# Shifting both stacks of SBUF tiles of an fp32r feed-forward kernel to round addresses

## The chip, the cores and the metric

One NeuronCore of a Trainium2 chip runs the program. The metric is the device time of one execution in microseconds (us). TensorE (PE) multiplies, VectorE (DVE) and ScalarE (ACT) work on single elements, GpSimd (POOL) fills constants, SyncE (SP) issues transfers. A matmul has two operands in SBUF: the stationary one, which a weight load (LDWEIGHTS, engine PEld) puts into the array, and the moving one, which streams through it column by column; the sum goes to PSUM.

## The reference

Linear attention without a softmax, then two feed-forward layers on 2304 tokens of 512 features:

```python
kv  = np.einsum('bhsd,bhse->bhde', k, v)          # batch 4, 8 heads, 576 positions, 64 wide
out = np.einsum('bhsd,bhde->bhse', q, kv)
x   = out / np.sqrt(np.mean(out * out, -1, keepdims=True) + 1e-06) * g_norm   # to (2304, 512)
h   = x @ w_in                                    # 512 to 2048
x   = (h * np.clip(h + 3.0, 0.0, 6.0) / 6.0) @ w_out
p   = domain_probs / (domain_probs.sum(-1, keepdims=True) + 1e-09)
for e in range(4):                                # experts: 512 to 1024 to 512
    out2 += p[:, e:e + 1] * (np.maximum(x @ w1[e], 0.0) @ w2[e])
```

## The kernel before, in words

Everything is float32. For the two feed-forward layers each operand is split into a high and a low part of type fp32r, and three products stand for one: high by high, high by low, low by high.

The work has three stages. The attention (to about 80 us) goes over eight pairs of a batch and half of its heads: q is transposed on PE (L208, `pq`), k and v are multiplied (L221, `kvp`), q by that product (L246, `po`), the result is normalized and transposed back (L304, `px`) into the tiles `xH` and `xL`. The first layer (to about 500 us) goes over 16 slices of 128 hidden features, grouped in units of 2, 4, 4 and 6, and five blocks of tokens (four of 512, one of 256): 12 matmuls of the input product (L333 to L335, moving `xH` or `xL`, stationary `w`), then 12 of the output product (L356, moving `gH` or `gL`, stationary `w`), three items late so that ACT and DVE can make `gH` and `gL` in between. The expert layer goes over three passes of 768 tokens, four experts and four groups of 256 hidden features; its input product is done with seven products instead of eight (L677, 384 columns, moving `xs`, stationary `win`), and the output product of the group before (L632, 512 columns, moving `wout`, stationary `g2`) fills in between.

SBUF is filled by two stacks. Pools open from the lower end in the order of the code, those with `side="right"` from the upper end downwards; a pool's tiles lie one behind the other, each rounded up to 32 bytes. So a pool's first byte is the sum of what was opened before it. The slices that the matmuls of the two feed-forward layers read begin at multiples of 512 bytes within their tile (128 weights, 384 or 512 columns, of 4 bytes each), so a whole tile has one residue. In the built program the first bytes within a partition are:

| tile | read by | role | first byte before (past a multiple of 512) | after |
|---|---|---|---|---|
| `ident`, `kvbd` | L208, L304; L246 | | 1152 (128); 2400, 3424 (352) | not moved |
| attention inputs in `accp` | L208, L221 | both | 4544 and on by 8192 (448) | 5120 and on (0) |
| `gH`, `gL` | L356 | moving | 45504 to 59840 (448) | 46080 to 60416 (0) |
| `xH`, `xL` | L333 to L335 | moving | 66368 to 131904 (320) | 66560 to 132096 (0) |
| `xs` | L677 | moving | 66368 to 125760 (320) | 66560 to 125952 (0) |
| `win` | L677 | stationary | 135136, 149472 (480) | 134144, 148480 (0) |
| `w` | L333 to L335, L356 | stationary | 163808 to 221152 (480) | 162816 to 220160 (0) |
| `g2` | L632 | stationary | 172000 to 212960 (480) | 171008 to 211968 (0) |
| `wout` | L632 | moving | 180192, 196576 (480) | 179200, 195584 (0) |

The order of the instructions on each engine is made when the program is built, by a scheduler that goes by its own estimate of times; a change in the first instructions can so move others later.

Of the kernel before, what the change touches and what calls it, by code (L numbers as in the profile page):

```python
# [8 lines left out]
F32 = mybir.dt.float32  # L9
# [8 lines left out]
def kernel(  # L18
# [18 lines left out]
    nc = tc.nc  # L37
# [3 lines left out]
    P = 128  # L41
# [18 lines left out]
    NA = NW - UNITS1[0]  # L60
    LAG = 3
    FMAX = 3.0e38

    const = ctx.enter_context(tc.tile_pool(name="const", bufs=1))
    accp = ctx.enter_context(tc.tile_pool(name="accp", bufs=NB))
    gp = ctx.enter_context(tc.tile_pool(name="gp", bufs=4))
    rp = ctx.enter_context(tc.tile_pool(name="rp", bufs=2))
    sp = ctx.enter_context(tc.tile_pool(name="sp", bufs=1))
    wp = ctx.enter_context(tc.tile_pool(name="wp", bufs=1, side="right"))
    xp = ctx.enter_context(tc.tile_pool(name="xp", bufs=1))  # L70

# [16 lines left out]
    def bank_b(shape, name):  # L88
        turn["b"] += 1
        pool, tag = (psc, "c") if turn["b"] % 6 == 0 else (psb, "b")  # L90
        return pool.tile(shape, F32, tag=tag, name=name)

    ident = const.tile([P, P], F32, name="ident")
    three = const.tile([P, 1], F32, name="three")
    gcol = const.tile([P, 1], F32, name="gcol")
# [162 lines left out]
    def att_rms(i):  # L258
# [6 lines left out]
        def scale():  # L265
            for g, tt in enumerate(banks(b)):
# [13 lines left out]
            lambda: nc.vector.scalar_tensor_tensor(  # L280
                out=w1_, in0=va, scalar=FMAX, in1=r0, op0=ALU.min, op1=ALU.mult),
            lambda: nc.vector.tensor_tensor(out=w1_, in0=w1_, in1=r0, op=ALU.mult),
# [424 lines left out]
    def run(g):  # L707
        return lambda: next(g, None)
# [20 lines left out]
    for k in range(NQ):  # L729
        ci, co = convert_in(k + 1) if 0 < k and k + 1 < NQ else iter(()), convert_out(k)  # L730
        side = [run(co), run(co), run(ci), run(ci), run(ci), run(ci), run(ci)]
# [41 lines left out]
```

## Time and profile before

| | |
|---|---|
| median of 3 runs | 1254.34 us (1251.5 to 1254.65) |
| profiled execution | 1252.49 us; span of its instructions 1250.7 us |
| mean granted clock of TensorE | 0.995 |
| PE, PEld busy | 1235.1, 1079.2 us |
| DVE, ACT, POOL busy | 767.6, 538.9, 1.3 us |
| matmuls | 6205 |

A record of a matmul lasts from its start until its last result is out, and the next one starts before that; so a PE that is always busy says nothing of how fast matmuls follow each other. The distance between starts does.

### The profile page before, as it was taken

The numbers are of one execution on the slowest core, as the hardware profiler recorded it, in microseconds if no ns is written. First come the engines' busy times: TensorE is split into PE (matmuls) and PEld (weight loads), VectorE is DVE, ScalarE is ACT, GpSimd is POOL, SyncE is SP. The second block draws the span as 40 slices with busy tenths as digits, with TensorE's granted clock in tenths as the row PEclk, the third lists the DMA queues.
The fourth block names the chain that finished last, engine by engine and source line by source line (L and its number), as shares of the span: only waits on it lengthen the run. The fifth ranks groups of instructions, "written<-read, shape, count | busy, mean of one in ns | idle before, by whom it ended". The sixth has DMA issues, their size and how long they took to land.

```text
span 1250.7 us, 15739 instructions
## 1 busy us (share of the span) xinstructions
PE 1235.1 (99%) x6205; PEld 1079.2 (86%) x6205; DVE 767.6 (61%) x1489; ACT 538.9 (43%) x1049; POOL 1.3 (0%) x10
## 2 busy tenths in 40 slices
PE   8899999999999999999999999999999999999998
PEld 6778888888888889999999999999999999999997
DVE  3989996693533465565656595656565856555553
ACT  5766753452322433333333353344444544444431
POOL 0000000000000000000000000000000000000000
PEclk9989999999999999999999999999999999999999
DMA  9932331120010002021111122122121222121111
GB/s 253 223 98 68 102 101 34 51 68 1 1 68 1 1 1 68 34 68 68 68 68 68 68 101 85 68 68 68 68 69 68 93 93 68 68 68 68 68 34 51
DMA packets 63897, 87.02 MB, mean 70 GB/s; under 512 B 5200, under 2 KB 47184, under 8 KB 63824
## 3 DMA queue, kind: packets, MB, share of 16 engines
q1 hardware_dynamic: 63664, 86.03, 22.3%
q8 instruction: 48, 0.79, 0.3%
q14 instruction: 25, 0.20, 0.1%
q10 hardware_dynamic: 160, 0.00, 0.0%
HBM read 81.30 MB, written 4.72 MB: 69 GB/s over the span
## 4 chain that ended last, share of the span: by engine, by line
PE 95%; DMA 2%; DVE 2%; ACT 1%; issue 0%; SPq 0%; DVEq 0%; ACTq 0%
PE po L632 32%; PE qa L677 16%; PE po L356 16%; PE qb L677 12%; PE ph L335 5%; PE ph L333 5%; PE ph L334 5%; DMA vin<-in_v_dram 2%; PE kvp L221 1%; PE po L246 1%; ACT qT L211 1%; PE px L304 0%; DVE ssq L255 0%; DVE xt L268 0%; ACT xt L252 0%
## 5 line engine op out<-in xcount | busy, mean ns | idle before, releaser
L632 PE MATMUL po<-wout,g 128*128 128x512 f32 x1728 | 435.9, 392 | 0.0
L632 PEld LDWEIGHTS po<-wout,g 128*128 128x128 f32 x1728 | 322.0, 188 | 54.3
L677 PE MATMUL qa<-xs,win 128*128 128x384 f32 x1152 | 234.7, 339 | 0.0
L677 PEld LDWEIGHTS qa<-xs,win 128*128 128x128 f32 x1152 | 206.8, 188 | 7.8
L356 PE MATMUL po<-gH,w 128*128 128x512 f32 (+1 forms) x640 | 196.4, 372 | 0.0
L677 PE MATMUL qb<-xs,win 128*128 128x384 f32 x864 | 176.3, 339 | 0.0
L677 PEld LDWEIGHTS qb<-xs,win 128*128 128x128 f32 x864 | 155.6, 188 | 11.5
L356 PEld LDWEIGHTS po<-gH,w 128*128 128x128 f32 x640 | 117.1, 188 | 23.0
L339 ACT ACTIVATE r<-ph,three 128x512 f32<-128x512 f32 (+1 forms) x80 | 51.6, 645 | 161.4 <-PE ph L335 161.0
L335 PE MATMUL ph<-xh,w 128*128 128x512 f32 (+1 forms) x320 | 120.0, 375 | 0.0
L333 PE MATMUL ph<-xh,w 128*128 128x512 f32 (+1 forms) x320 | 119.4, 373 | 0.0
L356 PE MATMUL po<-gL,w 128*128 128x512 f32 (+1 forms) x320 | 119.2, 373 | 0.0
L334 PE MATMUL ph<-xl,w 128*128 128x512 f32 (+1 forms) x320 | 119.2, 372 | 0.0
L340 DVE SCALAR_TENSOR_TENSOR r<-r,ph 128x512 f32<-128x512 f32 (+1 forms) x80 | 50.6, 632 | 108.5 <-ACT r L339 108.3
L652 DVE SCALAR_TENSOR_TENSOR g<-qb,g 128x384 fp32r<-128x384 f32 x48 | 26.8, 557 | 123.6 <-ACT g L651 123.6
L652 DVE SCALAR_TENSOR_TENSOR g<-qa,g 128x384 fp32r<-128x384 f32 x48 | 26.8, 557 | 95.3 <-ACT g L651 95.3
L546 ACT ACTIVATE win<-raw 128x512 fp32r<-128x512 f32 x96 | 45.1, 516 | 78.1 <-PE qa L677 78.1
L651 ACT ACTIVATE g<-cs 128x384 fp32r<-128x384 f32 x96 | 49.6, 517 | 59.1 <-DVE cs L698 54.3
L334 PEld LDWEIGHTS ph<-xl,w 128*128 128x128 f32 x320 | 60.2, 188 | 12.1
L333 PEld LDWEIGHTS ph<-xh,w 128*128 128x128 f32 x320 | 60.1, 188 | 11.8 <-issue 0.2
L356 PEld LDWEIGHTS po<-gL,w 128*128 128x128 f32 x320 | 60.2, 188 | 11.6
L335 PEld LDWEIGHTS ph<-xh,w 128*128 128x128 f32 x320 | 60.1, 188 | 11.3
(84 smaller groups left out, 1299.1 us busy)
## 6 DMA issues: line engine op xcount, KB each, us to landing
raw<-in_moe_w_dram SPq DMA_DIRECT2D x96, 512.0 KB, 4.3
raw<-in_moe_w_in_dram SPq DMA_DIRECT2D x16, 512.0 KB, 3.7
raw<-in_moe_w_out_dram SPq DMA_DIRECT2D x16, 512.0 KB, 3.5
qin<-in_q_dram SPq DMA_DIRECT2D x8, 576.0 KB, 13.8
kin<-in_k_dram SPq DMA_DIRECT2D x8, 576.0 KB, 13.9
vin<-in_v_dram SPq DMA_DIRECT2D x8, 576.0 KB, 13.2
out_dram<-acc SPq DMA_DIRECT2D x18, 256.0 KB, 2.0
dp<-in_moe_domain_probs_dram SPq DMA_DIRECT2D x1, 36.0 KB, 13.3
```

Of the source, the lines that this page charges most:

```text
L211: nc.scalar.activation(out=qv[:, :, :, j], in_=pq[half[j]].rearrange("p c s -> p s c"), func=AF.Copy)
L333: nc.tensor.matmul(ph, lhsT=w[:, 0, c, :], rhs=xH[t][:, c, :], start=(c == 0), stop=False)
L334: nc.tensor.matmul(ph, lhsT=w[:, 0, c, :], rhs=xL[t][:, c, :], start=False, stop=False)
L335: nc.tensor.matmul(ph, lhsT=w[:, 1, c, :], rhs=xH[t][:, c, :], start=False, stop=(c == KD - 1))
L339: nc.scalar.activation(out=r, in_=ph, func=AF.Relu, bias=three[:, 0:1])
L340: nc.vector.scalar_tensor_tensor(out=r, in0=r, scalar=6.0, in1=ph, op0=ALU.min, op1=ALU.mult)
L356: nc.tensor.matmul(po_t[u, t][o], lhsT=lhsT, rhs=rhs, start=(f == 0 and m == 0), stop=(f == UF[u] - 1 and m == 2))
L546: nc.scalar.activation(out=dst[0], in_=src, func=AF.Copy)
L632: nc.tensor.matmul(ps[i], lhsT=lhsT, rhs=w[:, f, y], start=(j == 0 and f == 0 and m == 0), stop=(j == FP - 1 and f == 1 and m == 2))
L651: nc.scalar.activation(out=g[0], in_=src, func=AF.Relu)
L652: nc.vector.scalar_tensor_tensor(out=g[1], in0=src, scalar=0.0, in1=g[0].bitcast(F32), op0=ALU.max, op1=ALU.subtract)
L677: nc.tensor.matmul(bank, lhsT=w[:, wy, AOP[m], c], rhs=xs[m][:, xy, c], start=first and n == 0, stop=n == 5, skip_group_check=True)
```

## The change

Two pools of padding are opened: one of 48 floats in the lower stack, one of 248 floats at the upper end. The pool `sp` of small tiles (four of 96 bytes) goes from behind `rp` to behind `const`, ahead of the padding. What follows in each stack begins at a multiple of 1024. POOL fills the two pads with zeros; nothing reads them. No other line changes; line numbers behind the new lines grow by 6.

```diff
+    PADL, PADR = 48, 248
 
     const = ctx.enter_context(tc.tile_pool(name="const", bufs=1))
+    sp = ctx.enter_context(tc.tile_pool(name="sp", bufs=1))
+
+    padl = ctx.enter_context(tc.tile_pool(name="padl", bufs=1))
+    padr = ctx.enter_context(tc.tile_pool(name="padr", bufs=1, side="right"))
     accp = ctx.enter_context(tc.tile_pool(name="accp", bufs=NB))
     gp = ctx.enter_context(tc.tile_pool(name="gp", bufs=4))
     rp = ctx.enter_context(tc.tile_pool(name="rp", bufs=2))
-    sp = ctx.enter_context(tc.tile_pool(name="sp", bufs=1))
     wp = ctx.enter_context(tc.tile_pool(name="wp", bufs=1, side="right"))
...
+    for pool, n in ((padl, PADL), (padr, PADR)):
+        nc.gpsimd.memset(pool.tile([P, n], F32, name="pad"), 0.0)
     ident = const.tile([P, P], F32, name="ident")
```

In the feed-forward layers PE's order is the same from the first blocks on. POOL's begins so after the change (`ident` is the identity for the transposes, `kvbd` a tile of the attention):

```order
L98 MEMSET pad 128x48
L98 MEMSET pad 128x248
masks.py:197 MEMSET ident 128x128
L453 MEMSET kvbd_110 128x256
masks.py:199 ISA
masks.py:199 AFFINE_SELECT ident<-ident 128x128
```

The two pads stand ahead of the identity; the rest is as before.

On PE, in the attention, the third pair of batch and heads stands so before (`pq` are the transposes of q, `kvp` the products of k and v, `po` those of q with them, `px` the transposes back):

```order
L246 MATMUL po<-kvbd_101,qT 128x128 x4
L221 MATMUL kvp<-vin,kin 128x128 x12
L246 MATMUL po<-kvbd_101,qT 128x128 x2
L246 MATMUL po<-kvbd_101,qT 64x128 x2
L304 MATMUL px<-ident,xt 128x128 x8
L208 MATMUL pq<-ident,qin 128x96 x8
L304 MATMUL px<-ident,xt 128x64 x2
```

And so after the change:

```order
L252 MATMUL po<-kvbd_111,qT 128x128 x3
L227 MATMUL kvp<-vin,kin 128x128 x12
L252 MATMUL po<-kvbd_111,qT 128x128 x3
L252 MATMUL po<-kvbd_111,qT 64x128 x2
L310 MATMUL px<-ident,xt 128x128 x8
L214 MATMUL pq<-ident,qin 128x96 x7
L310 MATMUL px<-ident,xt 128x64 x2
```

One `po` has passed behind the `kvp` group, and one `pq` behind the two short `px`.

At the end of the attention, PE's last `kvp` group stands so before (`ph` is the input product of the first layer):

```order
L304 MATMUL px<-ident,xt 128x64
L221 MATMUL kvp<-vin,kin 128x128 x12
L246 MATMUL po<-kvbd_100,qT 128x128 x8
L246 MATMUL po<-kvbd_100,qT 64x128 x2
L304 MATMUL px<-ident,xt 128x128 x6
L333 MATMUL ph<-xh_103,w 128x512
```

And so after the change:

```order
L310 MATMUL px<-ident,xt 128x64
L339 MATMUL ph<-xh_114,w 128x512
L227 MATMUL kvp<-vin,kin 128x128 x12
L252 MATMUL po<-kvbd_110,qT 128x128 x8
L252 MATMUL po<-kvbd_110,qT 64x128 x2
L310 MATMUL px<-ident,xt 128x128 x6
```

One `ph` now stands ahead of the last `kvp`. On SP nothing moves.

## Rows read from the trace of the kernel before

**Rows 1.** Chain that ended last: share of the span by engine.
```profile
PE 95%; DMA 2%; DVE 2%; ACT 1%; issue 0%; SPq 0%; DVEq 0%; ACTq 0%
```

**Rows 2.** Stretches: length, busy of PE, PEld, DVE, ACT, POOL; clock; DMA; GB/s.
```profile
72.00:78.80 6.80, 6.80 (x32) 6.80 (x33) 5.20 (x19) 1.93 (x4) 0.00 (x0) 0.50 0.03 12
79.00:1249.00 1170.00, 1167.84 (x5727) 1021.53 (x5726) 715.37 (x1341) 485.40 (x932) 0.00 (x0) 1.00 0.18 59
```

**Rows 3.** Timeline of PE, first layer: start, length, group.
```profile
298.12 0.40 PE L333 MATMUL ph<-xh,w 128*128 128x512 f32 x1
...
303.73 0.40 PE L333 MATMUL ph<-xh,w 128*128 128x512 f32 x1
```

**Rows 4.** Timeline of PE, end of the first layer: twelve of 256 columns lie between.
```profile
486.32 0.28 PE L356 MATMUL po<-gH,w 128*128 128x256 f32 x1
...
487.74 0.34 PE L684 MATMUL qb<-xs,win 128*128 128x384 f32 x1
```

**Rows 5.** Timeline of PE in the expert layer.
```profile
801.26 1.22 PE L677 MATMUL qb<-xs,win 128*128 128x384 f32 x6
...
803.38 1.55 PE L632 MATMUL po<-wout,g 128*128 128x512 f32 x6
804.77 1.22 PE L677 MATMUL qb<-xs,win 128*128 128x384 f32 x6
805.83 1.76 PE L632 MATMUL po<-wout,g 128*128 128x512 f32 x7
807.43 1.23 PE L677 MATMUL qb<-xs,win 128*128 128x384 f32 x6
...
809.55 2.01 PE L632 MATMUL po<-wout,g 128*128 128x512 f32 x8
811.40 1.23 PE L677 MATMUL qa<-xs,win 128*128 128x384 f32 x6
```

**Rows 6.** Timeline of PE at the end of the program.
```profile
1236.91 9.93 PE L632 MATMUL po<-wout,g 128*128 128x512 f32 x43
```

**Rows 7.** Groups of PE by form: count, busy us, mean ns, idle before.
```profile
L632 PE MATMUL po<-wout,g 128*128 128x512 f32 x1728 | 435.9, 392 | 0.0
L677 PE MATMUL qa<-xs,win 128*128 128x384 f32 x1152 | 234.7, 339 | 0.0
L677 PE MATMUL qb<-xs,win 128*128 128x384 f32 x864 | 176.3, 339 | 0.0
L356 PE MATMUL po<-gH,w 128*128 128x512 f32 x512 | 171.2, 396 | 0.0
L335 PE MATMUL ph<-xh,w 128*128 128x512 f32 x256 | 101.9, 398 | 0.0
...
L356 PE MATMUL po<-gH,w 128*128 128x256 f32 x128 | 25.2, 280 | 0.0
L333 PE MATMUL ph<-xh,w 128*128 128x256 f32 x64 | 18.1, 283 | 0.0
```

**Rows 8.** Groups of DVE by form.
```profile
L547 DVE TENSOR_TENSOR wout<-raw,wout 128x512 fp32r<-128x512 f32 x96 | 61.9, 686 | 0.8 <-ACT wout L546 0.8
...
L342 DVE TENSOR_TENSOR gL<-r,gH 128x512 fp32r<-128x512 f32 x64 | 44.0, 687 | 15.9 <-ACT gH L341 15.7
```

**Rows 9.** Timeline of POOL and PEld at the start.
```profile
0.73 0.20 POOL masks.py:197 MEMSET ident<- 128x128 f32 x1 [0.29 <-POOLq L757]
...
1.21 0.29 POOL masks.py:199 TENSOR_SCALAR_AFFINE_SELECT ident<-ident 128x128 f32<-128x128 f32 x1
...
5.85 0.23 PEld L208 LDWEIGHTS pq<-ident,qin 96*128 96x128 f32 x1 [0.28 <-issue]
```

**Rows 10.** Waits of PE: total us, times, longest.
```profile
PE kvp L221 <- DMA vin<-in_v_dram: 3.1, 3, 1.3
...
PE pq L208 <- DMA qin<-in_q_dram: 0.6, 1, 0.6
```

**Rows 11.** Groups of PE by form: the warm-up.
```profile
L441 PE MATMUL zp<-zero 128*128 128x512 bf16 x12 | 5.3, 632 | 1.2 <-DVE zero L436 1.2
```

## The prediction

> **What bounds the kernel now.** I read the chain that ended last first. TensorE makes up 95% of it, the transfers and the other engines a few per cent each [rows 1]. The table by stretches shows where: from 79 to 1249 us, 94% of the span, PE is busy for 1167.84 of 1170 us at a granted clock of 1.00, which is the 2.4 GHz level; before that lies a stretch of 6.8 us at 0.50, the 1.2 GHz level [rows 2]. In the long stretch PE waits for nobody, so only the spacing of its matmuls, start to start, can change the time there. Busy times don't give it, since a matmul's record overlaps the next one's; the timeline does, as the distance between two starts divided by the matmuls between them.
>
> In the first feed-forward layer, 24 matmuls of 512 columns (12 of L333 to L335, then 12 of L356) go from 298.12 to 303.73 us: 233.8 ns each [rows 3]. At 2.4 GHz, 512 columns are 213.3 ns, so 20.4 ns are excess. Twelve of 256 columns take 1.42 us, 118.3 ns each; 11.6 are excess over 106.7 [rows 4]. In the expert layer, twelve of L677 (384 columns, 160.0 ns) take 2.12 us, 176.7 each, excess 16.7. Three blocks of L632 (512 columns) take 1.39, 1.60 and 1.85 us for 6, 7 and 8: 4.84 us for 21, 230.5 ns each, excess 17.2 [rows 5]. And the last 43 of L632, with nothing between them, take 9.93 us less the last one's own 0.39: 42 distances of 227.1 ns, excess 13.8 [rows 6].
>
> So the same instruction, same shape and clock, with PE waiting for nothing, is spaced 233.8 ns in one layer and 227.1 in the other when it runs undisturbed. The table of first bytes above shows what differs. In L333 to L335 and L356 the moving operand begins at 320 or 448 past a multiple of 512 bytes, and the weights at 480. In L632 both begin at 480. In L677 it is 320 against 480, and the L632 blocks between them are slower than the undisturbed run. Equal beginnings go with the fast spacing, unequal ones with the slow.
>
> **The change part by part.** The pads and the moved pool compute nothing; they shift every matmul operand of both feed-forward layers to 0 past a multiple of 512. All pairs then begin alike, as only L632's do now. I take that the spacing follows the relation of the two beginnings, and that excess falls to L632's 13.8 ns.
>
> First layer, 512 columns: counts are 512 for L356 with gH and four groups of 256, 1536 in all [rows 7]. At 233.8 - 227.1 = 6.7 ns this is 10.3 us. 512-column L632: 1728, of which the last 36 already run at 227; 1692 x (230.5 - 227.1) = 5.8 us, if the blocks settle once their neighbours are of the same kind. L677: 1152 + 864 = 2016 [rows 7]. No row shows one with equal beginnings. Its ends are nothing and the full 6.7 ns (13.5 us); I take the excess of the nearest row, 16.7 - 13.8 = 2.9 ns, 5.8 us. 256 columns: 128 and four groups of 64, 384 matmuls; their excess of 11.6 is already under 13.8, so I take 0, with 6.7 ns (2.6 us) as the other end. All of this lies on PE's path; nothing covers it, and nothing else comes late: in the long stretch DVE is busy 715 and ACT 485 of 1170 us [rows 2], and a PE faster by 2% asks 2% more of them.
>
> DVE and ACT read and write the shifted tiles too. DVE's 512-column subtraction takes 687 ns on tiles at 448 (L342) and 686 on tiles at 480 (L547) [rows 8], so I price them at 0; a slower one would lie beside PE.
>
> The two pad memsets go ahead of the identity on POOL. That engine's 128x128 memset takes 0.20 us, so 48 and 248 columns are about 0.5 us together, and the identity ends at 2.0 us instead of 1.5. The first weight load that belongs to its reader on PE starts at 5.85 us [rows 9]: 0.
>
> The order moves in the attention only: one matmul of po, pq or ph passes to the other side of a neighbour at a handful of places. What ends the long waits there is DMA, v's 3.1 us and q's 0.6 [rows 10], and SP's order is unchanged. The ph that now stands ahead of the last kvp falls into such a wait. I take 0; the ends are the loss or gain of the stretch at half clock (6.8 us of work would have been 3.4 us, so 3.4 either way) and the waits on DMA (3.7 either way, since the loads' targets shift as well, and no row shows loads at other targets).
>
> Sum: 10.3 + 5.8 + 5.8 = 21.9 us. The profiled execution took 1252.49 us, 1.8 below the median of the three timed runs (1254.34) and inside their spread. 1252.5 - 21.9 = 1230.6, so I forecast 1231 us.
>
> The nearest thing to a matmul without excess is the warm-up of L441: 12 of 512 columns, 5.3 us from the first start to the last end, 0.63 the one, so 11 distances of 424.5 ns [rows 11], what 512 columns take at 1.2 GHz, though in bf16. The Trainium skill (TensorE: Matmul & The Clock Gate, section Wait — 56ns, not 53.3ns?) puts the spacing of back-to-back matmuls at the 2.4 GHz level at columns over clock plus about 2.5 ns. The trace disagrees for these operands: none of its rows comes under 13.8 ns of excess at 512 columns. By that rule all four kinds would fall to 215.8, 162.5 and 109.2 ns, and the sum would be 85 us, 1167 in place of 1231; that lies inside rival B and shares its chance.
>
> **The rivals.** A, no change: what makes L632 fast is not the beginnings. Both its operands lie in the upper stack, while the others read the moving one from the lower; the rows can't separate that from the residues. The shift moves the stacks by a few hundred bytes and leaves every tile in its stack. Then all spacings stay: 1252.5 us. The Trainium skill (SBUF — State Buffer, section Specifications (TRN2)) speaks for this: it gives SBUF lines of 16 bytes, and all beginnings before are multiples of 32, on a line already. The trace agrees only so far that 320 and 448 cost the same 233 to 234 ns; it doesn't explain 227.
>
> B, much faster: a beginning on a round address also spares what is left of the excess, because a stream that begins inside a larger unit of the memory reads one unit more. All excess gone would be 1536 x 20.4 + 1692 x 17.2 + 36 x 13.8 + 2016 x 16.7 + 384 x 11.6 ns = 31.3 + 29.1 + 0.5 + 33.7 + 4.5 = 99 us, 1153. For it: the excess is a property of the stream, as no wait is in it. Against it: L632, which begins 32 bytes off any multiple of 64, has the least, so rounder has not been better so far. Halfway between the forecast and this end is 1192.
>
> C, slower: that last fact taken at its word. 448 and 320 are multiples of 64, 480 is not; L632 is fast because its moving operand begins in the middle of a 64-byte unit, where it misses the unit that the weight load wants. After the shift all moving operands begin on multiples of 64, and L632 falls into the slow kind: 1692 x (233.8 - 230.5) + 36 x 6.7 ns = 5.8 us, the rest as it is: 1258.3. It decides if L632's undisturbed spacing rises above 230.5. For it: two slow residues that are multiples of 64 and one fast that isn't. Against it: the weights begin at 480 in every layer and move too, so a scheme by which only the moving operand counts must ignore them.
>
> **How the numbers follow.** The forecast has 0.5, A 0.2, B 0.15, C 0.12, and 0.03 are left for something unforeseen in the attention. The forecast's own range: its ends are 10.3 + 5.8 + 13.5 + 2.6 + 3.7 = 35.9 us of gain, 1217, and, if only the first layer gains while the attention loses 3.7, 6.6 us, 1246. To leave out no more than 2 in 10, the range runs from 1205, short of most of B, to 1258, at C. The measurement tells apart about 0.3%, 3.8 us. Faster has the forecast and B, 0.65; same has A, 0.20; slower C and the rest, 0.15.
>
> **What would show it.** Step one holds if 12 matmuls of L356 (L362 in the new numbering) are spaced 227 ns; the sum's largest term fails if they stay at 233. The L632 run at the end tells A and the forecast (227) from B (under 220) and C (over 230). L677 at 173 or less confirms the middle term; at 176.7 it is 0. The stretch at half clock after 72 us shows whether the attention took part. The forecast is wrong as a whole if PE is found waiting anywhere after 90 us.

## The result and the profile after

The changed kernel takes 1240.43 us, median of six runs (1237.4 to 1244.72), against 1254.32 us of six runs of the kernel before on the same chip (1251.5 to 1254.82): a ratio of 0.9902, 95% interval 0.9878 to 0.9926. The forecast was 1231 us in a range of 1205 to 1258. The profiled execution took 1240.1 us with a span of 1238.3, where the one before had 1250.7. Runs of one kernel differ by about 7 us, along with the mean granted clock of the span: of the changed kernel, one run had a span of 1235.6 us at 0.997 and another 1242.9 us at 0.990.

L333 is now L339, L356 is L362, L677 is L683, L632 is L638. The chain that ended last and the stretches by engine (columns as in [rows 2]) say that the bound is the same:

```profile
PE 95%; DMA 2%; DVE 1%; ACT 1%; issue 0%; SPq 0%
```

```profile
72.00:78.80 6.80, 6.76 (x35) 6.67 (x36) 5.47 (x17) 2.43 (x5) 0.00 (x0) 0.58 0.25 75
79.00:1236.00 1157.00, 1155.50 (x5724) 1017.26 (x5723) 713.29 (x1341) 485.56 (x932) 0.00 (x0) 1.00 0.18 59
```

PE is still busy without a gap after 79 us, at a granted clock of 1.00, the 2.4 GHz level. So the difference is again in the distances between starts. First layer, 24 matmuls of 512 columns from start to start, the counterpart of [rows 3]:

```profile
292.52 0.39 PE L339 MATMUL ph<-xh,w 128*128 128x512 f32 x1
...
297.96 0.39 PE L339 MATMUL ph<-xh,w 128*128 128x512 f32 x1
```

5.44 us for 24, 226.7 ns each, where it was 233.8. Twelve of 256 columns, against [rows 4]:

```profile
476.23 0.28 PE L362 MATMUL po<-gH,w 128*128 128x256 f32 x1
...
477.67 0.34 PE L690 MATMUL qb<-xs,win 128*128 128x384 f32 x1
```

1.44 us, 120.0 ns each, where it was 118.3. The expert layer, against [rows 5]:

```profile
790.21 1.23 PE L683 MATMUL qb<-xs,win 128*128 128x384 f32 x6
791.28 1.20 PE L683 MATMUL qa<-xs,win 128*128 128x384 f32 x6
792.32 1.55 PE L638 MATMUL po<-wout,g 128*128 128x512 f32 x6
793.71 1.21 PE L683 MATMUL qb<-xs,win 128*128 128x384 f32 x6
794.75 1.78 PE L638 MATMUL po<-wout,g 128*128 128x512 f32 x7
796.37 1.20 PE L683 MATMUL qb<-xs,win 128*128 128x384 f32 x6
797.41 1.20 PE L683 MATMUL qa<-xs,win 128*128 128x384 f32 x6
798.45 2.01 PE L638 MATMUL po<-wout,g 128*128 128x512 f32 x8
800.30 1.23 PE L683 MATMUL qa<-xs,win 128*128 128x384 f32 x6
801.37 1.78 PE L638 MATMUL po<-wout,g 128*128 128x512 f32 x7
```

Most products of six narrow matmuls now take 1.04 us, 173.3 ns each, but those behind a block of eight (790.21 and 800.30) take 1.07, 178.3 ns. The L638 blocks of 6, 7 and 8 take 1.39, 1.62 and 1.85 us: no faster than the 1.39, 1.60 and 1.85 before. The last 43 of L638, against the 9.93 us of [rows 6]:

```profile
1224.55 9.95 PE L638 MATMUL po<-wout,g 128*128 128x512 f32 x43
```

Over the whole trace, from the start of each matmul to the next, the means in ns are (without some ten distances over 260 ns in either trace, between 80 and 102 us, where the attention still mixes in):

```
                            before   after   number   change, us
first layer, 512 columns     233.5   227.2     1536    -9.8
first layer, 256 columns     119.0   119.4      384    +0.2
L677/L683, 384 columns       176.9   175.0     2016    -3.9
L632/L638, 512 columns       230.2   231.1     1728    +1.6
```

That is -11.9 us for a span that fell by 12.4. The starts along the way agree: the second `ph` starts 0.5 us earlier than before (80.81 against 81.34, the attention's part), the first matmul of the expert layer 10.1 us earlier (477.67 against 487.74 in [rows 4]), and the final run of L638 12.4 us earlier (1224.55 against 1236.91 in [rows 6]).

### The profile page after: what moved, and what is told of

The parts are those of the page before. It is cut to its first block, busy times and chain, and to the rows that moved or that the text cites. A ratio compares the mean times of both kernels' runs of the same rounds, so it can differ in the third digit from the quotient of the medians.

```text
span 1238.3 us, 15745 instructions
## 1 busy us (share of the span) xinstructions
PE 1223.4 (99%) x6205; PEld 1075.4 (87%) x6205; DVE 765.7 (62%) x1489; ACT 538.9 (44%) x1049; POOL 1.6 (0%) x12
## 4 chain that ended last, share of the span: by engine, by line
PE 95%; DMA 2%; DVE 1%; ACT 1%; issue 0%; SPq 0%
PE po L638 32%; PE qa L683 16%; PE po L362 16%; PE qb L683 12%; PE ph L339 5%; PE ph L340 5%; PE ph L341 5%; PE kvp L227 1%; DMA kin<-in_k_dram 1%; PE po L252 1%; DMA vin<-in_v_dram 1%; ACT qT L217 1%; PE px L310 1%; DVE ssq L261 0%; DVE xl L321 0%; DVE xt L274 0%
## 5 line engine op out<-in xcount | busy, mean ns | idle before, releaser
L638 PE MATMUL po<-wout,g 128*128 128x512 f32 x1728 | 437.4, 393 | 0.0
L638 PEld LDWEIGHTS po<-wout,g 128*128 128x128 f32 x1728 | 321.2, 188 | 54.7
L683 PE MATMUL qa<-xs,win 128*128 128x384 f32 x1152 | 232.2, 336 | 0.0
L683 PEld LDWEIGHTS qa<-xs,win 128*128 128x128 f32 x1152 | 205.1, 188 | 8.1
L362 PE MATMUL po<-gH,w 128*128 128x512 f32 (+1 forms) x640 | 193.6, 368 | 0.0
L683 PE MATMUL qb<-xs,win 128*128 128x384 f32 x864 | 174.7, 337 | 0.0
L683 PEld LDWEIGHTS qb<-xs,win 128*128 128x128 f32 x864 | 154.9, 188 | 12.4
L362 PEld LDWEIGHTS po<-gH,w 128*128 128x128 f32 x640 | 117.2, 188 | 20.1
L339 PE MATMUL ph<-xh,w 128*128 128x512 f32 (+1 forms) x320 | 118.4, 370 | 0.8 <-ACT qT L217 0.8
L341 PE MATMUL ph<-xh,w 128*128 128x512 f32 (+1 forms) x320 | 118.0, 369 | 0.0
L362 PE MATMUL po<-gL,w 128*128 128x512 f32 (+1 forms) x320 | 117.8, 368 | 0.0
L339 PEld LDWEIGHTS ph<-xh,w 128*128 128x128 f32 x320 | 60.5, 189 | 11.2 <-ACT qT L217 1.0
L362 PEld LDWEIGHTS po<-gL,w 128*128 128x128 f32 x320 | 60.3, 188 | 9.8
## 6 DMA issues: line engine op xcount, KB each, us to landing
qin<-in_q_dram SPq DMA_DIRECT2D x8, 576.0 KB, 13.3
```

The costliest lines, as they stand in the source:

```text
L339: nc.tensor.matmul(ph, lhsT=w[:, 0, c, :], rhs=xH[t][:, c, :], start=(c == 0), stop=False)
L341: nc.tensor.matmul(ph, lhsT=w[:, 1, c, :], rhs=xH[t][:, c, :], start=False, stop=(c == KD - 1))
L362: nc.tensor.matmul(po_t[u, t][o], lhsT=lhsT, rhs=rhs, start=(f == 0 and m == 0), stop=(f == UF[u] - 1 and m == 2))
L638: nc.tensor.matmul(ps[i], lhsT=lhsT, rhs=w[:, f, y], start=(j == 0 and f == 0 and m == 0), stop=(j == FP - 1 and f == 1 and m == 2))
L683: nc.tensor.matmul(bank, lhsT=w[:, wy, AOP[m], c], rhs=xs[m][:, xy, c], start=first and n == 0, stop=n == 5, skip_group_check=True)
```

## The experiments

"Relation" is the first byte of the moving operand less that of the stationary one, modulo 256. Before: -32 for L356, 96 for L333 to L335 and for L677, 0 for L632. After: 0 everywhere. Line numbers differ by a few from run to run; the tile names (`ph`, `po<-gH`, `qa` and `qb`, `po<-wout`) stay. Distances without a line beside them are computed from the starts in that run's trace.

**Equal beginnings without round ones.** Only the lower stack is padded, so that all operands begin at 480 past a multiple of 512.

```diff
-    PADL, PADR = 48, 248
+    PADL = 40
...
-    padr = ctx.enter_context(tc.tile_pool(name="padr", bufs=1, side="right"))
...
-    for pool, n in ((padl, PADL), (padr, PADR)):
+    for pool, n in ((padl, PADL),):
```

> Lower stack shifted so that all its tiles begin 480 bytes past a multiple of 512, upper stack left at 480: all pairs of operands begin alike, none on a round address. If the relation of the two beginnings sets the spacing, L356 (512 columns) is spaced 227 ns as in the changed kernel, L677 about 174, and the time is about 1240 us. If round addresses set it, L356 stays at 233 and the time at 1252 to 1257. If the moving operand's beginning alone counts, 480 is as good as it was for L632: 227 and about 1240, and only the next two runs tell it from the relation.

1242.91 us (1238.78 to 1245.51), ratio 0.9916 (0.9886 to 0.9946). The means are those of the changed kernel: first layer 227.2, L682 175.0, L637 231.1 ns. So neither round addresses nor a move of the upper stack is needed for the gain. Rival A and the "round" part of rival B fall. That the moving operand's beginning alone doesn't decide is shown only by the runs that follow.

**One stack alone, left and right.** In the first only the lower stack is shifted (relation +32 everywhere but in the output matmuls), in the second only the upper (relation 64 where 96 was, -64 where -32 was).

```diff
-    PADL, PADR = 48, 248
+    PADL = 48
...
-    padr = ctx.enter_context(tc.tile_pool(name="padr", bufs=1, side="right"))
...
-    for pool, n in ((padl, PADL), (padr, PADR)):
+    for pool, n in ((padl, PADL),):
```

> Lower pad alone: moving operands of L333 to L335, L356 and L677 at 0, all weights and both operands of L632 at 480 as before. By the relation nothing is gained: L356 at 233, about 1252 us. By the moving operand alone: L356 at 227, L677 at 173 to 174, about 1240 us. By the weights' beginning alone: 233, 1252 us.

The second is an edit of the kernel before, so `sp` stays behind `rp`:

```diff
+    PADR = 248
...
+    padr = ctx.enter_context(tc.tile_pool(name="padr", bufs=1, side="right"))
...
+    for pool, n in ((padr, PADR),):
+        nc.gpsimd.memset(pool.tile([P, n], F32, name="pad"), 0.0)
```

> Upper pad alone: weights and both operands of L632 at 0, moving operands of L333 to L335 at 320 and of L356 at 448 as before. By the relation nothing is gained: 233, about 1252 us. By the weights' beginning alone: L356 at 227, about 1240 us. By the moving operand alone: 233, and L632 as in the changed kernel.

Lower alone: 1245.42 us (1244.71 to 1246.72), ratio 0.994 (0.9923 to 0.9958). Its first layer is slow, as expected:

```profile
297.70 0.39 PE L338 MATMUL ph<-xh,w 128*128 128x512 f32 x1
...
303.31 0.39 PE L338 MATMUL ph<-xh,w 128*128 128x512 f32 x1
```

5.61 us for 24, 233.8 ns. But its output blocks, both of whose operands lie in the upper stack and had not moved, became faster:

```profile
798.32 1.22 PE L682 MATMUL qb<-xs,win 128*128 128x384 f32 x6
799.38 1.22 PE L682 MATMUL qa<-xs,win 128*128 128x384 f32 x6
800.44 1.52 PE L637 MATMUL po<-wout,g 128*128 128x512 f32 x6
801.80 1.22 PE L682 MATMUL qb<-xs,win 128*128 128x384 f32 x6
802.86 1.76 PE L637 MATMUL po<-wout,g 128*128 128x512 f32 x7
804.46 1.22 PE L682 MATMUL qb<-xs,win 128*128 128x384 f32 x6
```

1.36 us for 6 (226.7 ns), where it was 1.39; a 7 still takes 1.60. Over the trace the blocks run at 227.7 ns instead of 230.2, while the narrow ones (384 columns) stayed at 1.06 us (176.7 ns). Upper alone: 1241.47 us (1237.13 to 1244.15), ratio 0.9915 (0.9892 to 0.9937), although no pair of the first layer begins alike:

```profile
298.64 0.39 PE L337 MATMUL ph<-xh,w 128*128 128x512 f32 x1
...
301.39 0.39 PE L360 MATMUL po<-gH,w 128*128 128x512 f32 x1
...
304.18 0.39 PE L337 MATMUL ph<-xh,w 128*128 128x512 f32 x1
```

Twelve `ph` take 2.75 us and twelve `po` 2.79. Over the trace its L337 to L339 run at 229.5 ns and its L360 at 232.5, the narrow ones at 173.5, the blocks at 229.5. Both expectations of no gain missed. Equal or unequal is too coarse, and the output blocks depend on what stands between them.

**The relation by itself.** A stream of matmuls and nothing else; both beginnings go through 0 to 480 in steps of 32 bytes, 15 matmuls of 512 columns a pair.

```diff
+    for s in range(0, 512, 32):
+        for r in range(0, 512, 32):
+            ps = group(512, r, s, 15)
+    for n in (384, 256):
+        for r, s in ((0, 0), (448, 480), (320, 480), (480, 480), (0, 256), (0, 64), (64, 0), (480, 0)):
+            ps = group(n, r, s, 24)
```

> Leaves the whole task out and only measures: 256 groups of 15 fp32r matmuls of 512 columns, each group with its own beginnings of the moving and the stationary operand, both in steps of 32 bytes from 0 to 480 past a multiple of 512; then some groups of 384 and 256 columns. The output is not the reference's. By the relation the 16 groups with equal beginnings are spaced 227 ns and the others 233 or more (perhaps only those that differ by an odd multiple of 32). By round addresses only the group 0, 0 is at 227. By the moving operand alone the spacing is the same along a column of the grid, by the weights alone along a row.

Distances in ns, mean of the last nine, for two of the sixteen stationary beginnings:

```
moving begins at    0     32     64     96    128    160    192    224    256    288 ...   448    480
stationary at 0   226.7  233.6  228.9  234.0  232.8  234.3  233.6  232.9  226.7  233.6 ... 233.6  232.9
stationary at 480 233.6  228.9  234.0  232.9  234.3  233.6  232.9  226.7  233.6  228.9 ... 232.9  226.7
```

The other fourteen rows are the same one, shifted. The spacing follows the relation modulo 256, with a fast value at 0 only and a half fast one at 64. At 384 columns it is 173.3 (relations 0, -32 and 64) or 176.7 (96 and -64); at 256 columns 120.0 (0 and 96) or 118 (-32, 64 and -64): there equal beginnings are the slower kind. This accounts for the first layer of the upper stack alone: 64 in L337 to L339 (228.9 in the grid, 229.5 in the kernel), -64 in L360 (233.6 and 232.5).

**Block lengths.** The changed kernel with its blocks at other lengths.

```diff
-        fill(8)
+        fill(6)
         product(qb, 6, False)
...
-        fill(6)
+        fill(8)
         product(qb, 5, False)
...
-        fill(7)
+        fill(8)
         product(qb, 3, False)
...
-        fill(8)
+        fill(6)
```

> The changed kernel with the second layer's filler blocks (output matmuls, 512 columns) at lengths 6, 8, 8, 6 and 8 per quad instead of 8, 6, 7, 8 and 7; addresses as in the changed kernel. In the changed kernel the products xs6 and xs4 ran at 178.3 ns a matmul and xs5, xs3, xs1 at 173.8 to 174.1. Theory H (what was run just before decides: a block of 8 leaves a bad phase, blocks of 6 or 7 do not): xs6 and xs4 now follow blocks of 6 and fall to 174.0; xs5, xs3 and xs1 follow blocks of 8 and rise to 178.3; the mean of all narrow products goes from 175.0 to 175.6, +1 us in all. Theory T (the tile or its place decides): xs6 and xs4 stay at 178.3, the rest at 174. Both: the wide blocks still begin 229, 233, 236, 224, 231, 236 ns.

```profile
790.25 1.21 PE L683 MATMUL qb<-xs,win 128*128 128x384 f32 x6
791.30 1.20 PE L683 MATMUL qa<-xs,win 128*128 128x384 f32 x6
792.34 2.01 PE L638 MATMUL po<-wout,g 128*128 128x512 f32 x8
794.19 1.23 PE L683 MATMUL qb<-xs,win 128*128 128x384 f32 x6
795.26 2.01 PE L638 MATMUL po<-wout,g 128*128 128x512 f32 x8
797.11 1.23 PE L683 MATMUL qb<-xs,win 128*128 128x384 f32 x6
```

Every product behind a block of eight takes 1.07 us: xs5, xs3 and xs1 went from 174 to 178.3 ns, and xs6 and xs4 from 178.3 to 174.0 (xs6 is the product at 790.25, xs5 the one at 794.19, xs3 the one at 797.11). What ran just before decides, not the tile. The only run's time, 1241.51 us, can't tell the +1 us that was expected.

**The switch between widths by itself.** The expert layer's pattern alone on the chip, each pair of relations twice (`narrow` issues six matmuls of 384 columns, `wide` as many of 512 as it is told).

```diff
+    for d512 in range(0, 256, 32):
+        for d384 in range(0, 256, 32):
+            for rep in range(2):
+                for n, m in ((1, 8), (2, 6), (1, 7), (2, 8), (1, 7)):
+                    for _ in range(n):
+                        narrow(d384)
+                    wide(m, d512)
```

> A measurement by itself (the output is not the reference's): TensorE runs the second layer's pattern of six 384-column matmuls and blocks of 6 to 8 matmuls of 512 columns, with nothing else on the chip's engines; moving minus stationary beginning is stepped by 32 bytes from 0 to 224 for the 384-column ones and, apart from that, for the 512-column ones, two rounds of the pattern each (the second is read). Theory S (switching between widths itself starts a transient, whose course depends on the relation of the narrow matmuls): at (384: 0, 512: 0) the wide blocks show 231 ns and the series 229, 233, 236, 224, 231, 236, 228, 233 of the changed kernel; at (384: +32, 512: 0) about 227.6, at (384: +64, 512: 0) about 229.3 with the narrow ones at 173.5. Theory O (the transient comes from other work in the kernel: drains, DMA or the other engines): the wide blocks are at 226.7 everywhere where the 512-column relation is 0, whatever the narrow relation is.

At relations 0 and 0 it repeats the changed kernel's blocks of 8 and 6 to a hundredth of a us:

```profile
24.58 2.01 PE L69 MATMUL o<-mv,st 128*128 128x512 f32 x8
26.43 2.27 PE L79 MATMUL q<-mv,st 128*128 128x384 f32 x12
28.54 1.55 PE L69 MATMUL o<-mv,st 128*128 128x512 f32 x6
29.93 1.21 PE L79 MATMUL q<-mv,st 128*128 128x384 f32 x6
```

A block of eight starts 229, 233, 236, 224, 231, 236, 228, 233 ns apart, in the kernel and here. So no drain, transfer or other engine is in it: after narrow matmuls the wide ones need more than a block to settle, even where every operand begins alike. (In the last 43 of L638 the series goes on with 231 and is at 226.7 from the tenth on.) I call this settling the transient. It doesn't take a switch of widths: in the grid's kernel, whose first 24 matmuls all have 512 columns and relation 0, nine distances are 426.7 ns and the tenth 406, and after it come 233, 236, 224, 231, 236, 228, 233, 231 and then 226.7. The means, with what the kernels showed (narrow and wide, ns):

```
narrow relation  wide relation   alone            in a kernel
       0              0          175.0  231.2     175.0  231.1  (after)
      96              0          176.9  230.3     176.9  230.2  (before)
      32              0          176.7  227.7     176.7  227.7  (lower stack alone)
      64              0          173.4  229.5     173.5  229.5  (upper stack alone)
     -32              0          173.9  226.9     174.0  226.9  (xs at 224, below)
```

**Shifting the narrow weights.** From the table, relation 64 looked better than 0 for the narrow ones; here `win` is moved by a 64-byte pad.

```diff
-    PADL, PADR = 48, 248
+    PADL, PADR, PADW = 48, 248, 16
...
+    padw = ctx.enter_context(tc.tile_pool(name="padw", bufs=1, side="right"))
+    nc.gpsimd.memset(padw.tile([P, PADW], F32, name="padw"), 0.0)
     winp = ctx.enter_context(tc.tile_pool(name="winp", bufs=2, side="right", reuse_waits="tile"))
```

> The changed kernel with a 64-byte pad in front of the pool of the second layer's input weights, so that only their relation to the moving operand changes, from 0 to +64; first layer and output matmuls stay at relation 0. Theory S (relations of narrow and wide matmuls decide, also in the transients): narrow 175.0 to 173.5 (-3 us), output blocks 231.0 to 229.3 (-2.9 us), first layer unchanged at 227.2; about 6 us below the changed kernel, 1234 us. Theory R (relation 0 is the best there is everywhere, and what the kernel with only the upper stack shifted showed in the second layer came from something else in it): the narrow ones go to 177 and the time to about 1244 us.

1240.33 us (1236.31 to 1243.33), ratio 0.99 (0.988 to 0.992): as the changed kernel, and not the 6 us less that were expected.

```profile
794.47 1.22 PE L685 MATMUL qb<-xs,win 128*128 128x384 f32 x6
795.52 1.78 PE L640 MATMUL po<-wout,g 128*128 128x512 f32 x7
797.15 1.20 PE L685 MATMUL qb<-xs,win 128*128 128x384 f32 x6
```

The narrow ones run at 174.0, the blocks at 231.5 and not at 229.5, beginning 241, 224, 231, 236. So the relation within one matmul isn't the whole of it: moving the weights by -64 differs from moving the stream by +64, though both have relation 64. What also differs is how the operands on the two sides of a switch stand to each other; that this is the cause is not shown.

**Shifting the narrow stream: a better version.** The last row of the table, put into the kernel: the `xs` tiles begin at 224 modulo 256 (PADX is 56 columns of 4 bytes), all else stays at 0.

```diff
-    PADL, PADR = 48, 248
+    PADL, PADR, PADX = 48, 248, 56
...
+    padx = ctx.enter_context(tc.tile_pool(name="padx", bufs=1))
+    nc.gpsimd.memset(padx.tile([P, PADX], F32, name="padx"), 0.0)
     xsp = ctx.enter_context(tc.tile_pool(name="xsp", bufs=1, reuse_waits="tile"))
...
-            xs[m] = pool.tile([P, 2, 2, TH], F32R, tag=XSHOME.get(m, f"xs{m}"), name=f"xs{m}")
+            n = PADX if m in XSHOME else 0
+            x = pool.tile([P, n + 4 * TH], F32R, tag=XSHOME.get(m, f"xs{m}"), name=f"xs{m}")
+            xs[m] = x[:, n:].rearrange("p (y c t) -> p y c t", y=2, c=2)
```

> The changed kernel with the second layer's moving operand (the xs tiles) moved to begin at 224 modulo 256 bytes, all else at 0: relation -32 for the narrow products, 0 for the output matmuls and the first layer. Theory S (what the measurement by itself showed holds in the kernel, whatever the other engines do): narrow 173.9 ns instead of 175.0 (-2.2 us), output blocks 226.9 instead of 231.0 (-7.1 us), first layer at 227.2 as in the changed kernel; in all -9 us, 1231 us. Theory O (in the kernel other work brings the transient): the output blocks stay at 230 or more and the time at 1238 or more.

1230.35 us (1228.08 to 1233.37), ratio 0.9816 (0.9791 to 0.984), faster than the changed kernel (0.9878 to 0.9926) beyond both intervals.

```profile
790.10 1.20 PE L687 MATMUL qa<-xs,win 128*128 128x384 f32 x6
791.14 1.52 PE L642 MATMUL po<-wout,g 128*128 128x512 f32 x6
792.50 1.21 PE L687 MATMUL qb<-xs,win 128*128 128x384 f32 x6
793.54 1.75 PE L642 MATMUL po<-wout,g 128*128 128x512 f32 x7
795.13 1.21 PE L687 MATMUL qb<-xs,win 128*128 128x384 f32 x6
796.18 1.20 PE L687 MATMUL qa<-xs,win 128*128 128x384 f32 x6
797.22 1.98 PE L642 MATMUL po<-wout,g 128*128 128x512 f32 x8
799.03 1.21 PE L687 MATMUL qa<-xs,win 128*128 128x384 f32 x6
```

Blocks of 6, 7 and 8 take 1.36, 1.59 and 1.81 us; over the trace they run at 226.9 ns and the narrow ones at 174.0, the first layer unchanged at 227.2. The transient is gone: the first distance in a block is 228 ns, all others are 226.7.

**Whose operands.** Two pairs of operands alternate; either the two of one matmul begin alike, or the moving one and the next matmul's weights do.

```diff
+    for n in (512, 384):
+        for d in range(32, 256, 32):
+            group(n, ((0, 0), (d, d)), 24)
+            group(n, ((d, 0), (0, d)), 24)
```

> A measurement by itself (the output is not the reference's): two pairs of operands alternate, 24 matmuls a group, 512 and then 384 columns, for d from 32 to 224 bytes. In one group each matmul's own two operands begin alike, (0, 0) and (d, d), so that the stationary operand of the matmul after it stands d off the moving one; in the other the own ones stand d apart, (d, 0) and (0, d), and the moving one begins like the stationary operand of the next. Theory OWN (the two operands of one matmul): the first kind runs at 226.7 ns for every d, the second at 233 to 234 (229 at 64 and 192). Theory NEXT (the moving operand against the weights that are loaded meanwhile for the matmul after it): the second kind runs at 226.7, the first at 233 to 234.

At 512 columns, from the sixth distance on, the first kind ran at 231.7 to 236.7 ns over the seven values of `d`, the second at 229.7 to 231.9; none reached 226.7. At 384 columns it was 175.4 to 176.7 and 173.3 to 176.7. Both theories fall as put: neither relation alone is enough. What inside the chip the relation acts on stays open.

## Why the prediction was right, and where it wasn't

The main step held: spacing follows the relation of the two beginnings, and equal ones give 227 ns at 512 columns. That it is a relation, and not the address or the stack, is shown by the kernel with all beginnings at 480 and by the grid. The time alone would not have shown it: the range of 1205 to 1258 us also holds the 1252.5 of rival A.

*First layer.* Forecast 10.3 us, measured 9.8 (233.5 to 227.2 ns). Right.

*256 columns.* Forecast 0, measured 0.2 us lost: equal beginnings are the slower kind there, 120.0 against the 118 that L356 had at -32. The settled excess is now about 13.3 ns at all three widths, over 213.3, 160.0 and 106.7 ns.

*L677.* Forecast 5.8 us from a range of 0 to 13.5, measured 3.9. The settled spacing is 173.3, 3.6 ns less than before and so a larger gain than the 2.9 taken; but two of seven products follow a block of eight and run at 178.3, and three follow a shorter one and run at 173.8 to 174.0. The block-length run shows that cause.

*L632 blocks.* Forecast 5.8 us, measured 1.6 us lost; this step failed. It rested on "if the blocks settle once their neighbours are of the same kind". They don't settle. Before, too, these blocks had relation 0 and ran at 230; I laid this to unlike neighbours, but the switch from 384 to 512 columns starts the transient even where all relations are 0, as the pattern alone shows, and it lasts longer than a block. The neighbours do count, but the other way: the version with `xs` at 224 gets 7.3 us (231.1 to 226.9) by giving them an *unequal* relation. That this version comes out at 1230.35 us, next to the forecast of 1231, is chance.

*Attention, pads, DVE and ACT.* Costed at 0. The attention gave 0.5 us, which says little: in the eight traces of whole kernels its end (the start of the second `ph`) lies between 78.6 and 83.4 us. The pads run on POOL at 0.73 us, before the first transpose:

```profile
0.73 0.38 POOL L98 MEMSET pad<- 128x48 f32 x2 [0.29 <-POOLq L763]
1.04 0.20 POOL masks.py:197 MEMSET ident<- 128x128 f32 x1
```

The subtractions on DVE keep their time against [rows 8]:

```profile
L553 DVE TENSOR_TENSOR wout<-raw,wout 128x512 fp32r<-128x512 f32 x96 | 61.8, 685 | 0.8 <-ACT wout L552 0.8
...
L348 DVE TENSOR_TENSOR gL<-r,gH 128x512 fp32r<-128x512 f32 x64 | 44.0, 688 | 16.1 <-ACT gH L347 15.8
```

Against the sum of 21.9 us, the span fell by 12.4; of the 9.5 missing, 7.4 are the L632 step and 1.9 the L677 step; the rest is 0.5 in the first layer and 0.2 at 256 columns, less the attention's 0.5.

*The rivals.* A (no change) falls with the first layer at 227. B (all excess gone) falls: nothing in any run settles under 226.7 at 512 columns. The Trainium skill (TensorE: Matmul & The Clock Gate, section Wait — 56ns, not 53.3ns?) has about 2.5 ns over columns by clock; for these fp32r operands no settled spacing here leaves less than about 13 ns at 512 or 384 columns. C (relation of the moving operand to 64-byte units) falls, as the grid's rows differ by a shift only; that the blocks became 0.9 ns slower is the transient, since their settled spacing is still 226.7.

## What to carry to other kernels

On a stream of fp32r matmuls that bounds the time, read start-to-start distances by tile pair, and set the two operands' first bytes against each other modulo 256: 3% at 512 columns lay in that, and a pad of a few hundred bytes buys it. Padding to round addresses isn't needed. Where two widths alternate, measure the pattern by itself with the relation of each as a parameter, and shift there the operand that you will shift in the kernel: here it gave the means of five kernels to 0.1 ns, those of the best one ahead of its run, but not those of the kernel whose weights were moved in place of the stream. The best setting was not the tidy one.

## What the runs showed that was not expected

The spacing in a stream depends on what ran up to nine matmuls earlier: after a switch from 384 to 512 columns with all relations 0 the distances go through the same series each time, to within a nanosecond, and a block of eight instead of six or seven sends the next narrow product from 174 to 178 ns. The same series, from its second value on, stands at the start of the grid's kernel, where all matmuls have 512 columns, right after the spacing drops from 426.7 ns. So equal beginnings give the fast spacing only to a stream that has had time to settle. And the relation doesn't say all: the same relation, 64, reached by moving the stream or by moving the weights, gave blocks of 229.5 and 231.5 ns.
